# 74 of 4096 attention tiles get their exponential from VectorE's polynomial instead of ScalarE, and LayerNorm's squares go by halves

## The chip, the cores and the metric

The kernel runs on one core of a Trainium2 chip. The core has five engines with a queue of instructions each, which run side by side and wait for one another through semaphores: TensorE (PE in the profile, with its weight loads as PEld), VectorE (DVE), ScalarE (ACT), GpSimd (POOL) and SyncE (SP), whose queue issues most of the DMAs. On-chip memory is SBUF, with 128 partitions, and PSUM, with 8 banks of 128 x 512 fp32, into which TensorE writes. The metric is device time in microseconds of one launch, as the median of several.

## The reference

Two kinds of layer alternate, A, B, A, B, each adding to the stream `x` of 2048 x 1024 bf16, 32 heads of 32.

```python
x = A_x
x = x + _A_ref(_layernorm(x, axis=-1), A_wqkv, A_w_phi, A_wo)   # linear attention
x = x + _B_ref(_layernorm(x, axis=-1), B_wqkv, B_wo)            # softmax attention
x = x + _A_ref(_layernorm(x, axis=-1), A_wqkv, A_w_phi, A_wo)
x = x + _B_ref(_layernorm(x, axis=-1), B_wqkv, B_wo)
...
scores = jnp.einsum("bhqd,bhkd->bhqk", q, k) * (Dh ** -0.5)
p = _softmax(scores, axis=-1)
o = jnp.einsum("bhqk,bhkd->bhqd", p, v)
```

`_A_ref` computes features `softmax(q w_phi)` and `softmax(-q w_phi)`, the same for k, sums `phi_k` times v over the sequence, and divides `phi_q kv` by `phi_q z`. The bulk of the arithmetic on elements is the softmax of `_B_ref`: 32 heads x 2048 x 2048 exponentials, twice.

## The kernel before, in words

`x` stays in SBUF, transposed (`xT`: features on partitions), in four chunks of 512 positions. One A and one B are called a layer here, so the program has two layers.

**Attention** (`attention`). A unit is one tile of scores: 128 keys by 512 queries of one head. A layer has 2048 of them. The order is fixed by `turns`: a turn is one group of four heads (`g`, 8 of them) and one chunk of queries (`qc`, 4), 32 turns a layer, first chunks 0 and 1 alternating over the groups and then chunks 2 and 3. A turn has two halves (`pp`), each with 8 steps `d` of 4 units (`j`, one per row group of TensorE). The units of a layer are taken three at a time:

- L937: three score matmuls (32 rows of the array each) into three PSUM banks, 0 to 2 and 3 to 5 by turns.
- L943: one ScalarE `Exp` over 128 x 1536, from PSUM into one of five SBUF buffers of class `E`.
- L972: for two units, four matmuls on 32 columns each, `v` and a block of ones times the exponentials, accumulated over the half in PSUM bank 6 (`acc`). There is only one `acc`.
- L986: at the end of a half VectorE copies `acc` to SBUF. Two DMAs (L1012 and its neighbour) bring the denominators into place, VectorE takes reciprocals (L1016, four a turn) and multiplies (L1020, two a turn).

Bank 7 (`FIL`) serves everything else that must go on under attention: the projections of later head groups (`b_k`, `b_q`, `q_away`, `b_v`), the output projection (`b_o`, in the second layer `b_last`), and at the end of layer 0 three chunks of the next A (LayerNorm and `a_keys` with `alone=True`). These use the column-tiled matmul of L401, whereas the stages outside attention use the full array, L397.

**LayerNorm** (`layernorm`). Where it is not `alone`: ScalarE squares `xT` in four instructions of 128 x 1024 (L454), each as soon as its quarter of the features is there; ones-matmuls sum `x` and the squares; then L474 and L476 (mean squared, mean), L477 (variance), L479 and L481 (logarithm, exponential), and four pairs of L487 and L491 that write the normalised chunk.

**Order.** `Sched` is a list scheduler that runs while the program is built. Every operation has a priority (`base + 10 * turn + ...`), a modelled duration and buffers taken from one SBUF arena and the PSUM banks with a quota per class. What comes out is one fixed order of instructions for each engine. Where TensorE has nothing to start and has worked less than 75% of the last 3.4 us of the plan, the planner puts in four matmuls of ones times `xT` into bank 7 (`idle`), but only if bank 7 is free. Their result is used by nobody.

Of the kernel before, what the change touches and what calls it, by code (L numbers as in the profile page):

```python
# [9 lines left out]
ACT = mybir.ActivationFunctionType  # L10
ALU = mybir.AluOpType
AX = mybir.AxisListType
BF16 = mybir.dt.bfloat16
F32 = mybir.dt.float32

EPS_LN = 1e-5
# [16 lines left out]
class Op:  # L33
    __slots__ = ("eng", "dur", "lat", "fn", "bufs", "prio", "mode", "ndep", "out", "t", "start", "seq")

    def __init__(self, eng, dur, lat, fn, bufs, prio, mode, seq):
        self.eng, self.dur, self.lat, self.fn, self.bufs = eng, dur, lat, fn, bufs
        self.prio, self.mode, self.seq = prio, mode, seq
        self.ndep, self.out, self.t, self.start = 0, [], 0.0, None

# [5 lines left out]
class Sched:  # L46
    def __init__(self, sbuf_bytes, quota):
        self.ops = []
        self.quota = quota
        self.live = {}  # L50
        self.free = [(0, sbuf_bytes)]
        self.bank_used = [False] * 8
        self.peak = 0
        self.total = sbuf_bytes
        self.queue = {}
        self.idle = None

# [85 lines left out]
    def run(self):  # L143
# [17 lines left out]
        front = 0  # L161
        recent = []
        started = {}
        for o in self.ops:
# [3 lines left out]
        while left:  # L168
            moved = False
            for e in engines:  # L170
# [24 lines left out]
                if e == "PE":  # L195
                    recent.append((t, t + pick.dur))
                d = pick.dur
                if pick.mode is not None:
# [3 lines left out]
                pick.start = t  # L202
                if pick.fn is not self.idle:
                    started[pick.prio] = started.get(pick.prio, 0) + 1
# [44 lines left out]
SPELL = 3.4  # L249
KEEP = 0.75  # L250


def act_us(n):
    return n / 1200 + 0.064
# [10 lines left out]
def kernel(  # L265
# [18 lines left out]
    assert D == 1024 and S % C512 == 0  # L284
    inv_sqrt_dh = float(DH**-0.5)

# [15 lines left out]
    onesD = const.tile([P, P], BF16, tag="onesD")  # L302
    ones_bf = const.tile([P, DH], BF16, tag="ones")
    J_bf = const.tile([P, P], BF16, tag="J")
    ident = const.tile([P, P], BF16, tag="ident")
# [8 lines left out]
    nc.vector.memset(onesD[:], 1.0 / D)  # L314
    nc.vector.memset(ones_bf[:], 1.0)
    nc.vector.memset(J_bf[:], 0.0)
    nc.vector.memset(eps[:], EPS_LN)
# [70 lines left out]
    def csl(c):  # L388
        return slice(c * C512, (c + 1) * C512)
# [48 lines left out]
    def deps_x(c):  # L438
        return list(xdone[c])

    def layernorm(c, prio, banks, alone=False):

# [5 lines left out]
        parts = [deps_x(c)[2 * i:2 * i + 2] for i in range(4)]  # L448
        for h in range(2 if alone else 4):
            hs = slice(4 * h, 4 * h + 4)  # L450
            if not alone:
                hs = slice(2 * h, 2 * h + 2)
                halves.append(op(
                    "ACT", act_us(1024), lambda hs=hs: nc.scalar.activation(  # L454
                        out=xv()[:, hs, :], in_=xT[:, hs, csl(c)], func=ACT.Square),
                    parts[h], [xb], prio))
# [9 lines left out]
        m = mmgroup(mb, mv, lambda po: onesD[:], lambda po: xT[:, po, csl(c)], (), parts, [], prio)  # L466
        q = mmgroup(qb, qv, lambda po: onesD[:], lambda po: xv()[:, po, :], [m],
                    [halves[0], None, halves[1], None] if alone else halves, [xb], prio + 0.01)
        if alone:
# [348 lines left out]
    def b_q(g, c, prio, w, banks):  # L818
        wb, ww, wd = w
        xb, xv, fin = xnB[c]  # L820
        pb, pv = ps("fil", banks)
        m = mmg2(pb, pv, lambda po: ww()[:, po, :], lambda po: xv()[:, po, :], fin, wd, [xb, wb], prio)
        q_b, q_v = sb("q2", 2, C512)
        cp = op("DVE", dve_us(512), lambda: nc.vector.tensor_scalar(
            out=q_v()[:, 0, :], in0=pv(), scalar1=inv_sqrt_dh, scalar2=None, op0=ALU.mult), [m], [pb, q_b], prio)
        return q_b, q_v, q_swap(q_b, q_v, cp, prio)
# [6 lines left out]
    def q_away(g, c, prio, w, banks):  # L833
# [6 lines left out]
        cp = op("DVE", dve_us(512), lambda: nc.vector.tensor_scalar(  # L840
            out=a_v(), in0=pv(), scalar1=inv_sqrt_dh, scalar2=None, op0=ALU.mult), [m], [pb, a_b], prio)
        return dma(prio, lambda: nc.sync.dma_start(out=qd_v[:, c - 2, g, :], in_=a_v()), [cp], [a_b], kb=128)
# [64 lines left out]

    def attention(base, kT, vT, q_of, gate):

# [4 lines left out]
        ]  # L914
        first = {}
        ex_of, e_of = {}, {}
        n = 0
        i = 0
        while i < len(units):
# [14 lines left out]
            def sfn(grp=grp, s_v=s_v):  # L934
# [8 lines left out]
            ex = op("ACT", act_us(w * C512), lambda s_v=s_v, e_v=e_v, w=w: nc.scalar.activation(  # L943
                out=e_v()[:, 0:w * C512], in_=s_v(), func=ACT.Exp), [so], [s_b, e_b], prio - 3)
            for x, u in enumerate(grp):
# [5 lines left out]
        if True:  # L951
            for qc, g in turns:
                T = []
                end = (qc, g) == turns[-1]
                for pp in range(2):
                    a_b, a_v = ps("acc", [(6,)])
                    last = None
                    for d in range(8):
                        prio = base + 10 * pos[(qc, g)] + 5 * pp + 0.5 * d
                        for u in range(2):  # L960
# [18 lines left out]
                            if e_of[us[1]][0] is not ebs[0]:  # L979
                                ebs.append(e_of[us[1]][0])  # L980
                            last = op("PE", 0.225, fn, flat([last, ex_of[us[0]], ex_of[us[1]], v_done[kc % 4]]),
                                      [a_b, v_b, *ebs], prio - 1, mode="c")
                    if end and pp:
                        break
# [67 lines left out]
    for layer in range(2):  # L1052
# [73 lines left out]
        oTs, last_s = attention(at, kT, vT, q_of, gate)  # L1126
        if last:
# [50 lines left out]
    sch.idle = idle  # L1178

    for o in sch.run():  # L1180
        o.fn()
# [30 lines left out]
```

## Time and profile before

| | us |
|---|---|
| median of 3 runs (2552.54 to 2556.16) | 2554.63 |
| the profiled execution | 2554.77 |
| its span | 2553.0 |
| ACT busy | 2181.1 |
| PE busy | 2329.9 |
| DVE busy | 1144.7 |

PE's busy time is modelled from pipelined matmuls and includes the `idle` ones. From about 420 to 1340 us the program is in the first attention, from about 1620 us to the end in the second; before each lies a stage of A with the projections of B.

### The profile page before, as it was taken

To read this page: it belongs to the slowest core of one execution; us is meant where nothing else is said; L and a number is where in the kernel's file an instruction comes from. 1 tells how busy PE (TensorE), PEld (TensorE's weight loads), DVE (VectorE), ACT (ScalarE), POOL (GpSimd) and SP (SyncE) were. 2 spreads that over 40 slices of the span, in tenths; PEclk is the share of its full clock that TensorE was granted. 3 is DMA by queue.
4 is the path that set the end of the run, shared out by engine and by line. 5 is a ranking of instruction groups with operands and counts; after the bars stand their busy time and mean duration, and the time that the engine had idled before them with its cause. 6 is when DMAs were issued, how large, how long until landed. Compare 5 with 4: busy or idle time off the path is not lost.

```text
span 2553.0 us, 60236 instructions
## 1 busy us (share of the span) xinstructions
PE 2329.9 (91%) x26714; PEld 882.9 (35%) x26780; DVE 1144.7 (45%) x1632; ACT 2181.1 (85%) x1945; POOL 25.8 (1%) x72
## 2 busy tenths in 40 slices
PE   6899999999898998899898999999998898889888
PEld 3443443333322333333333344333332233333333
DVE  5997653333322245655646766333333222212124
ACT  5325647999999999999996555799999999999998
POOL 0000000000000000000000000000000000000000
PEclk9999999999998999999999999999999899999999
DMA  9020011111121222222323001111121011001000
GB/s 215 1 75 1 5 38 46 35 35 44 40 64 38 53 53 70 75 64 69 117 71 102 1 5 38 36 45 35 37 67 30 20 33 43 20 18 33 18 20 26
DMA packets 185270, 117.21 MB, mean 46 GB/s; under 512 B 103345, under 2 KB 175025, under 8 KB 184241
## 3 DMA queue, kind: packets, MB, share of 16 engines
q1 hardware_dynamic: 183952, 111.26, 16.3%
q8 instruction: 209, 3.42, 0.6%
q10 hardware_dynamic: 1056, 2.10, 0.2%
q14 instruction: 53, 0.43, 0.1%
HBM read 62.46 MB, written 15.73 MB: 31 GB/s over the span
## 4 chain that ended last, share of the span: by engine, by line
ACT 53%; PE 26%; issue 11%; DVE 8%; SPq 1%; DMA 1%; ACTq 0%; DVEq 0%; another core or an unknown queue 0%
ACT arena L943 51%; PE psum L397 13%; PE psum L401 4%; PE psum L972 3%; PE psum L937 3%; DVE arena L593 2%; DVE arena L602 1%; PE psum L757 1%; DVE arena L491 1%; DVE arena L487 1%; ACT arena L589 1%; SPq L432 1%; DVE arena L596 1%; DVE arena L639 0%; PE psum L702 0%
## 5 line engine op out<-in xcount | busy, mean ns | idle before, releaser
L943 ACT ACTIVATE arena<-psum 128x1536 bf16<-128x1536 f32 (+1 forms) x1366 | 1844.4, 1560 | 29.1 <-PE psum L937 23.6
L972 PE MATMUL psum<-arena 128*32 128x512 bf16 x4096 | 712.7, 390 | 13.5 <-ACT arena L943 11.6
L972 PE MATMUL psum<-arena,ones_bf 128*32 128x512 bf16 x4096 | 714.1, 391 | 0.0
L937 PE MATMUL psum<-arena 32*128 32x512 bf16 x4096 | 537.8, 387 | 135.5 <-ACT arena L943 127.3
L401 PE MATMUL psum<-arena 128*32 128x512 bf16 x8256 | 582.5, 382 | 13.8 <-DVE arena L840 2.1
L397 PE MATMUL psum<-arena 128*128 128x512 bf16 x1973 | 468.6, 382 | 26.5 <-DVE arena L491 5.5
L937 PEld LDWEIGHTS <-arena 32*128 32x128 bf16 x4096 | 181.7, 91 | 643.8 <-issue 632.1
L401 PEld LDWEIGHTS <-arena 128*32 128x32 bf16 x8256 | 213.0, 96 | 222.1 <-issue 74.2
L397 PEld LDWEIGHTS <-arena 128*128 128x128 bf16 x2032 | 193.2, 98 | 268.5 <-issue 50.2
L986 DVE COPY arena<-psum 128x512 f32<-128x512 f32 x126 | 86.9, 690 | 431.3 <-PE psum L972 428.0
L972 PEld LDWEIGHTS <-arena 128*32 128x32 bf16 x4096 | 167.7, 94 | 283.0 <-issue 259.3
L1016 DVE RECIPROCAL arena<-arena 128x128 f32<-128x128 f32 x248 | 212.8, 913 | 85.7 <-DMA arena<-arena 82.8
L816 DVE CAST arena<-psum 128x512 bf16<-128x512 f32 x112 | 77.4, 691 | 283.5 <-PE psum L401 280.3
L972 PEld LDWEIGHTS <-ones_bf 128*32 128x32 bf16 x4096 | 162.1, 94 | 70.1 <-issue 58.7
L401 PE MATMUL psum<-xT,onesD 128*32 128x512 bf16 x2172 | 179.7, 382 | 0.6 <-DVE xT L876 0.3
L589 ACT ACTIVATE arena<-psum 128x512 bf16<-128x512 f32 x80 | 42.6, 603 | 110.7 <-PE psum L397 58.8
L454 ACT ACTIVATE arena<-xT 128x1024 bf16<-128x1024 bf16 x52 | 54.6, 1060 | 73.2 <-DVE xT L792 59.2
L719 ACT ACTIVATE arena<-psum 128x512 bf16<-128x512 f32 x128 | 69.8, 598 | 38.2 <-PE psum L397 32.2
L602 DVE TENSOR_TENSOR arena<-psum,arena 128x1024 bf16<-128x1024 f32 x64 | 78.3, 1224 | 43.6 <-PE psum L401 39.4
L1020 DVE TENSOR_TENSOR arena<-arena 64x512 bf16<-64x512 f32 x124 | 85.0, 686 | 10.1 <-PE psum L972 5.7
L487 DVE TENSOR_TENSOR arena<-xT,arena 128x1024 f32<-128x1024 bf16 x64 | 77.7, 1218 | 22.7 <-ACT arena L476 22.4
L593 DVE TENSOR_REDUCE arena<-arena 128x32 f32<-128x1024 bf16 x64 | 77.6, 1213 | 19.1 <-ACT arena L589 15.0
(89 smaller groups left out, 1051.8 us busy)
## 6 DMA issues: line engine op xcount, KB each, us to landing
arena<-arena SPq DMA_DIRECT2D x124, 128.0 KB, 2.3
arena<-in_A_wqkv_dram SPq DMA_DIRECT2D x10, 1024.0 KB, 5.7
arena<-in_B_wqkv_dram SPq DMA_DIRECT2D x32, 256.0 KB, 3.3
arena<-arena SPq DMA_DIRECT2D x256, 32.0 KB, 1.9
arena<-in_B_wo_dram SPq DMA_DIRECT2D x32, 256.0 KB, 3.1
arena<-wd_k SPq DMA_DIRECT2D x8, 1024.0 KB, 6.1
arena<-in_A_wo_dram SPq DMA_DIRECT2D x4, 1024.0 KB, 6.5
arena<-in_B_wqkv_dram SPq DMA_DIRECT2D x4, 1024.0 KB, 5.5
```

The lines of the kernel that those rows point to most:

```text
L397: nc.tensor.matmul(out_, lhsT=lhsT, rhs=rhs, start=start, stop=stop, skip_group_check=True)
L401: nc.tensor.matmul(out_[ks, :], lhsT=lhsT[:, ks], rhs=rhs, start=start, stop=stop, tile_position=(0, 32 * k), skip_group_check=True)
L487: s1 = op("DVE", dve_us(1024), lambda pr=pr, w_v=w_v: nc.vector.tensor_tensor(out=w_v(), in0=xT[:, pr, csl(c)], in1=m_v().unsqueeze(1).to_ ...
L593: red = op("DVE", dve_us(1024), lambda ev=ev, sv=sv: nc.vector.reduce_sum(out=sv(), in_=ev().rearrange("p s (h d) -> p (s h) d", d=DH), ax ...
L602: ml = op("DVE", dve_us(1024), lambda vpv=vpv, wv_=wv_, sv=sv: nc.vector.tensor_tensor(out=wv_()[:, :, :, 0:DH], in0=vpv().rearrange("p (h ...
L816: return op("DVE", dve_us(512), lambda: nc.vector.tensor_copy(out=dst(), in_=src()), [dep], bufs, prio)
L937: nc.tensor.matmul(out=s_v()[:, x * C512:(x + 1) * C512], lhsT=kT[g][1]()[r, pp, d * P:(d + 1) * P], rhs=q_of[(qc, g)][1]()[r, (pp + j // ...
L943: ex = op("ACT", act_us(w * C512), lambda s_v=s_v, e_v=e_v, w=w: nc.scalar.activation(out=e_v()[:, 0:w * C512], in_=s_v(), func=ACT.Exp), ...
L972: nc.tensor.matmul(out=a_v()[col:col + 32, :], lhsT=v_v()[:, kc % 4, o:o + DH] if what == 0 else ones_bf[:], rhs=ev()[:, x * C512:(x + 1) ...
L986: cp = op("DVE", dve_us(512), lambda t_v=t_v, a_v=a_v: nc.vector.tensor_copy(out=t_v(), in_=a_v()), [last], [a_b, t_b], prio - 4)
L1016: rc = [op("DVE", 128 * 8 / 960 + 0.12, lambda b=b, d_v=d_v, r_v=r_v: nc.vector.reciprocal(out=r_v()[:, b * P:(b + 1) * P], in_=d_v()[:, b ...
L1020: s = [op("DVE", dve_us(512), lambda a=a, b=b, k=k, o_v=o_v, r_v=r_v, T=T: nc.vector.tensor_tensor(out=o_v()[a, :], in0=T[k][1]()[a, :], i ...
```

## The change

- **`exp_dve`.** 37 pairs of units (keys `d` = 2 and 3 of one half, `j` = 3) leave the groups of three. For each unit TensorE writes the scores alone into bank 7 (class `xs`), and VectorE computes the exponential: with the scores scaled by 1/(4 ln 2), the exponential is 2 to the power of four times the score. Adding 1.5 * 2^21 rounds to quarters, a subtraction leaves the rest, a clamp, a conversion to int32 gives the bits of the power of two, and four multiply-adds evaluate a polynomial of degree four in the rest. That is 10 VectorE instructions a pair: four of 128 x 512 with PSUM as a source (L949, L952, twice each), two of 128 x 1024 in SBUF alone (L955, L958), and four of 128 x 1024 with two sources (L963 three times, L966). The result goes into a buffer `E1` of which there are three.
- **`EXTRA`** says which: in layer 0 one pair in each of turns 12 to 16; in layer 1 one pair in turns 8 to 16, 20, 24 and 28, and two pairs in turns 17 to 19, 21 to 23, 25 to 27 and 29. That makes 10 and 64 units.
- `q` is scaled by 1/(4 ln 2) more, and ScalarE's `Exp` gets the constant `scale=4 ln 2`, no bias.
- **`idle_acc`.** Where bank 7 is taken and an accumulation in bank 6 is open, the planner may fill with four matmuls of zeros into `acc`.
- **LayerNorm.** Squares go in two instructions of 128 x 2048, and squares and sums wait for the whole chunk (`deps_x(c)`), except in the one LayerNorm that begins layer 1's A (`n=4`), which keeps quarters.

```diff
+ROUND = 1.5 * 2**21
+LEAD = 5.0
+EXTRA = (lambda i: [(i % 2, 2)] if 12 <= i < 17 else [],
+         lambda i: [(0, 2), (1, 2)] if 16 < i < 30 and i % 4 else [(i % 2, 2)] if 8 <= i < 30 else [])
...
-                    if worked < KEEP * SPELL and not self.live.get("fil", 0) and not self.bank_used[7]:
+                    if worked >= KEEP * SPELL:
+                        pass
+                    elif self.bank_used[7]:
+
+                        if accum:
+                            pick = Op("PE", MM, LAT["PE"], self.idle_acc, (), 0.0, "c", 0)
+                            left += 1
+                    elif not self.live.get("fil", 0):
...
-    def layernorm(c, prio, banks, alone=False):
+    def layernorm(c, prio, banks, alone=False, n=2):
...
-        for h in range(2 if alone else 4):
-            hs = slice(4 * h, 4 * h + 4)
+        for h in range(n):
+            hs = slice(8 // n * h, 8 // n * h + 8 // n)
...
-                    parts[h], [xb], prio))
+                    parts[h] if n == 4 else deps_x(c), [xb], prio))
...
+    def exp_dve(qc, g, pp, d, prio, kT, q_of):
+        u_b, u_v = sb("xu", 2, C512, dt=F32)
+        g_b, g_v = sb("xg", 2, C512, dt=F32)
+        x_b, x_v = sb("xx", 2, C512, dt=F32)
+        e_b, e_v = sb("E1", 2, C512)
+        r = slice(96, 128)
+        gs = []
+        for k in range(2):
+            s_b, s_v = ps("xs", FIL)
...
+            so = op("PE", MM, sfn, flat([kT[g][2][(d + k) // 2], q_of[(qc, g)][2]]),
+                    [s_b, kT[g][0], q_of[(qc, g)][0]], prio, mode="r")
+            uo = op("DVE", dve_us(512), lambda k=k, s_v=s_v: nc.vector.tensor_scalar(
+                out=u_v()[:, k, :], in0=s_v(), scalar1=POW2_D, scalar2=ROUND, op0=ALU.add, op1=ALU.add),
+                [so], [s_b, u_b], prio + 0.01)
+            gs.append(op("DVE", dve_us(512), lambda k=k, s_v=s_v: nc.vector.scalar_tensor_tensor(
+                out=g_v()[:, k, :], in0=u_v()[:, k, :], scalar=ROUND, in1=s_v(), op0=ALU.subtract, op1=ALU.subtract),
+                [uo], [s_b, u_b, g_b], prio + 0.01))
+        wo = op("DVE", 1024 / 1920 + 0.15, lambda: nc.vector.tensor_scalar(
+            out=u_v(), in0=u_v(), scalar1=ROUND - 31.5, scalar2=ROUND + 32.0, op0=ALU.max, op1=ALU.min),
+            gs, [u_b], prio + 0.02)
+        wo = op("DVE", 1024 / 1920 + 0.15, lambda: nc.vector.tensor_scalar(
+            out=u_v().bitcast(I32), in0=u_v(), scalar1=ROUND - 31.75, scalar2=float(2**25),
+            op0=ALU.subtract, op1=ALU.mult), [wo], [u_b], prio + 0.02)
+        last = gs
+        for i, c in enumerate(POW2_C):
+            last = [op("DVE", dve_us(1024), lambda i=i, c=c: nc.vector.scalar_tensor_tensor(
+                out=x_v(), in0=(x_v() if i else g_v()), scalar=c, in1=g_v(), op0=ALU.add, op1=ALU.mult),
+                last, [g_b, x_b], prio + 0.02)]
+        eo = op("DVE", dve_us(1024), lambda: nc.vector.scalar_tensor_tensor(
+            out=e_v(), in0=x_v(), scalar=POW2_0, in1=u_v(), op0=ALU.add, op1=ALU.mult),
+            [wo, *last], [x_b, u_b, e_b], prio + 0.02)
...
             ex = op("ACT", act_us(w * C512), lambda s_v=s_v, e_v=e_v, w=w: nc.scalar.activation(
-                out=e_v()[:, 0:w * C512], in_=s_v(), func=ACT.Exp), [so], [s_b, e_b], prio - 3)
+                out=e_v()[:, 0:w * C512], in_=s_v(), func=ACT.Exp, scale=4 * math.log(2)),
+                [so], [s_b, e_b], prio - 3)
...
-            xnA[c] = layernorm(c, base + 10 * c - 9 if base + c else -16.0, ANY)
+            xnA[c] = layernorm(c, base + 10 * c - 9 if base + c else -16.0, ANY, n=4 if layer else 2)
...
+    def idle_acc():
+        for k in range(4):
+            nc.tensor.matmul(psum[32 * k:32 * k + 32, 6 * C512:7 * C512], lhsT=zero[:], rhs=xT[:, 0, 0:C512],
+                             start=False, stop=False, tile_position=(0, 32 * k), skip_group_check=True)
+    sch.idle_acc = idle_acc
```

More of the change, by code (lines that the diff above doesn't have):

```diff
@@ L33 @@
 class Op:
-    __slots__ = ("eng", "dur", "lat", "fn", "bufs", "prio", "mode", "ndep", "out", "t", "start", "seq")
+    __slots__ = ("eng", "dur", "lat", "fn", "bufs", "prio", "mode", "ndep", "out", "t", "start", "seq", "accum")
     def __init__(self, eng, dur, lat, fn, bufs, prio, mode, seq):
@@ L38, in __init__ @@
         self.prio, self.mode, self.seq = prio, mode, seq
-        self.ndep, self.out, self.t, self.start = 0, [], 0.0, None
+        self.ndep, self.out, self.t, self.start, self.accum = 0, [], 0.0, None, None
 LAT = {"PE": 0.25, "ACT": 0.2, "DVE": 0.1, "POOL": 0.2, "SP": 2.0, "AQ": 2.0}
@@ L315 @@
     nc.vector.memset(ones_bf[:], 1.0)
+    nc.vector.memset(zero[:], 0.0)
     nc.vector.memset(J_bf[:], 0.0)
@@ L911, in attention @@
+    def attention(base, kT, vT, q_of, gate, extra):
         units = [
@@ L914, in attention @@
         ]
-        first = {}
         ex_of, e_of = {}, {}
+        for qc, g in turns:
+            for pp, d in extra(pos[(qc, g)]):
+                eo, (e_b, e_v) = exp_dve(qc, g, pp, d, base + 10 * pos[(qc, g)] + 5 * pp + 0.5 * d - LEAD, kT, q_of)
+                for k in range(2):
+                    ex_of[(qc, g, pp, d + k, 3)] = eo
+                    e_of[(qc, g, pp, d + k, 3)] = (e_b, e_v, k)
+        units = [u for u in units if u not in ex_of]
         n = 0
@@ L1125 @@
                     q_of[(qc, g)] = q_back(g, qc, at + 10 * pos[(qc, g)] - 12, away)
-        oTs, last_s = attention(at, kT, vT, q_of, gate)
+        oTs, last_s = attention(at, kT, vT, q_of, gate, EXTRA[layer])
         if last:
```

33 lines of the change are left out of this document (23 added, 10 removed), and 3 rows, old and new, of the table QUOTA.

## The prediction, written before the changed kernel ran

> **What bounds the kernel now.** I read the page's busy line and slices first, then the chain that ended last, then busy time by stretch, then the waits of the second attention (1620 us to the end) and of the slow spot at 740 to 800 us, and last the groups for the durations.
>
> ```profile
> PE 2329.9 (91%) x26714; PEld 882.9 (35%) x26780; DVE 1144.7 (45%) x1632; ACT 2181.1 (85%) x1945; POOL 25.8 (1%) x72
> ...
> DVE  5997653333322245655646766333333222212124
> ACT  5325647999999999999996555799999999999998
> ...
> ACT 53%; PE 26%; issue 11%; DVE 8%; SPq 1%; DMA 1%; ACTq 0%; DVEq 0%; another core or an unknown queue 0%
> ```
> ```profile
> 760.00:770.00 10.00, 7.63 (x65) 1.70 (x57) 0.69 (x1) 9.18 (x8) 0.00 (x0) 0.74 0.06 13
> 770.00:780.00 10.00, 8.41 (x61) 1.92 (x58) 0.69 (x1) 8.78 (x7) 0.00 (x0) 0.50 0.01 2
> 1850.00:2475.00 625.00, 557.70 (x7449) 194.67 (x7445) 166.54 (x222) 622.29 (x463) 0.00 (x0) 0.99 0.11 31
> ```
> ```profile
> 2436.42 2.64 ACT arena L943 x2
> 2439.11 2.63 ACT arena L943 x2
> 2441.78 2.65 ACT arena L943 x2
> ...
> 380.31 1.06 ACT arena L454
> ```
> ```profile
> PE psum L937 <- ACT arena L943: 66.5, 270, 0.6
> PE psum L972 <- ACT arena L943: 5.4, 23, 0.4
> ...
> PE psum L937 <- ACT arena L943: 6.5, 15, 0.6
> ```
> ```profile
> L943 ACT ACTIVATE arena<-psum 128x1536 bf16<-128x1536 f32 x1364 | 1842.5, 1560 | 29.1 <-PE psum L937 23.6 <-PE psum L972 3.5 <-issue 1.3
> L1016 DVE RECIPROCAL arena<-arena 128x128 f32<-128x128 f32 x248 | 212.8, 913 | 85.7 <-DMA arena<-arena 82.8 <-ACT arena L943 2.4
> L986 DVE COPY arena<-psum 128x512 f32<-128x512 f32 x126 | 86.9, 690 | 431.3 <-PE psum L972 428.0 <-DMA arena<-arena 3.0
> L487 DVE TENSOR_TENSOR arena<-xT,arena 128x1024 f32<-128x1024 bf16 x64 | 77.7, 1218 | 22.7 <-ACT arena L476 22.4
> L687 DVE SCALAR_TENSOR_TENSOR arena<-arena,hl 128x512 bf16<-128x512 bf16 x32 | 24.0, 751 | 1.2
> L840 DVE TENSOR_SCALAR arena<-psum 128x512 bf16<-128x512 f32 x32 | 22.1, 691 | 85.3 <-PE psum L401 80.1 <-DMA arena<-arena 5.0
> L686 DVE CAST arena<-arena 128x512 bf16<-128x512 f32 x32 | 13.6, 425 | 38.8 <-ACT arena L775 34.3 <-ACT arena L742 4.4
> ```
>
> In both attentions ScalarE is full and VectorE mostly idle. The stretch 1850 to 2475 holds 44 of the copies of L986, so it is turns 8 to 29 of layer 1: ScalarE works 622.3 of 625 us, VectorE 166.5 (7.6 us a turn). The chain there is exponentials end to end, two groups in 2.69 us. TensorE waits for ScalarE before the scores (66.5 us in all, 0.6 us at most), and its 558 us include filling. So a unit costs 2.69/6 = 0.448 us of the end time, and every unit taken off ScalarE there gives that back unless something else comes late.
>
> **The change, part by part.**
>
> *Exponentials that leave ScalarE.* 74 units x 0.448 = **-33.2 us** (28.7 in layer 1, 4.5 in layer 0). All lie in turns where ScalarE is the bound. The constant scale costs nothing: L589 has one and takes 603 ns, as L719 does (598) and the scale-free Square of L474 (598).
>
> *The polynomial on VectorE.* Per pair: L949 twice as L840, 2 x 0.69; L952 twice between L477 (0.686) and L687 (0.751), 2 x 0.72; four of 1024 elements with two sources as L487, with up to 0.065 more as L687 has over L477, 4 x 1.25; L955 and L958 have no row. Their bounds are 0.425 (L686, fp32 from SBUF, one source, half the elements) and 1.22 (L487); L686 runs at about half the time per element of L477, which over 1024 elements gives about 0.69, and it is their nearest row, so 2 x 0.69. Sum 9.2 us, ends 8.5 and 10.5. 37 x 9.2 = 340 us of VectorE. Beside ScalarE that costs nothing as long as a turn of VectorE is shorter than a turn of ScalarE. With two pairs: 7.6 + 18.4 = 26.0 us against 60 x 0.448 = 26.9; with one: 16.8 against 27.8. So ten turns of layer 1 are 97% full on VectorE, and only the one-pair turn after each three leaves slack, 11 us. Three `E1` buffers let VectorE run ahead by no more than three pairs; in the changed order most pairs end between the copies of the two halves before their use.
>
> What queues behind: VectorE works in order, so copies of `acc` (L986, now L1057), reciprocals and the evacuations of bank 7 wait for the polynomial step in front, 1.25 us at most each. 39 of the 126 copies stand directly behind a polynomial step. For the copy waits the next half's accumulation on TensorE (one `acc`), and behind that, in TensorE's order, the next scores. Two score buffers give ScalarE 1.34 us of cover beyond the group it is in. I take 0.6 us lost in each of the ten two-pair turns: **+6 us**. Ends: 0 (all covered) and +22 (10.5 us a pair makes such turns 28.6 us, 1.7 over, ten times, plus 5 for copies).
>
> *Scores for VectorE.* 74 single matmuls of at most 0.39 us each (the length of one in L937) against 25 groups of three less, and 792 fills of four matmuls for 519 by the two orders, at 0.216 us each (the page's chain has 32 of L401 in 1.73): about +75 us of TensorE. Cost 0: they lie in TensorE's waits for ScalarE and in place of each other. Without that cover a single score would be some 0.3 us late, 74 times, under the 22 us above.
>
> *Fills while bank 7 is taken.* At 740 to 800 us bank 7 is held, nothing fills, and the granted clock falls to 0.50; ScalarE loses 0.82 and 1.22 us in the two slices shown. The slices of 10 us with a clock under 0.95 (700, 760 to 800, 1910 to 1930, 1980 to 2020) lose 7.4 us of ScalarE together. The zero matmuls should hold the clock where `acc` is open. I take a little over half, **-4 us**; ends -7.4 and +3 (new low spots where the copy is late, no accumulation is open and bank 7 is held). The Trainium skill (TensorE: Matmul & The Clock Gate, "HAM oscillation") says that the clock halves after an idle window of about 3.4 us. By it nothing would have throttled here, since TensorE waited 0.6 us at most, this term would be 0 and the sum 2528.6. The trace disagrees: 0.50 at 770 to 780 with matmuls every 1.4 us, and the measurement decides.
>
> *LayerNorm.* Two squares of 2048 cost about 1.9 each (1.06 plus 1024 elements at the 0.82 ns that L943's 1560 and 1139 for 512 fewer give), back to back 3.7 for 3.9. But all now follow the last addition, where only one of 1.06 did: 2.7 us later. That is on the path for the last chunk of each layer's B LayerNorm (the chain has 380.31 L454, and attention cannot run freely before 400 us); the others lie under the next chunk's queries. In return, in the order of the changed kernel six exponentials stand in that gap instead of three, 4.0 us of ScalarE's later work, two of them between the mean and the logarithm. I take 0 for each gap, ends -2 and +6 for both, and **+1 us** for the kernel's start, where the first LayerNorm must wait for all eight loads (ends -3 and +5; the weights' folding runs there until 41 us).
>
> SP's and GpSimd's queues issue the same instructions, 739 and 74, and nothing is moved past them but by the planner's own shifts.
>
> **Sum** against the profiled execution's own 2554.77 (the median is 2554.63, the same): 2554.8 - 33.2 + 6 - 4 + 1 = 2524.6, so 2524 us.
>
> **The rivals.**
> - *VectorE bounds the two-pair turns.* For it: 97%, and steps without a row. If L955 and L958 take 1.22 us, a pair costs 10.3, the ten turns 28.2 us for 26.9 (+13), with copies late +5; -33.2 + 18 - 2 + 1 gives 2538, up to 2549. Against it: the one-pair turns' slack. By the rows a unit is ten times dearer on VectorE (4.6 us for 0.448), which matters only from the point where VectorE is full. The Trainium skill (ScalarE: Activation LUTs, "Rules for kernel authors") calls ScalarE the only option for `exp`; it speaks against this change and leads to this rival.
> - *All of it goes through*, and the clock holds: -33.2 - 7.4 - 1, 2513. For it: TensorE's waits for ScalarE all over 1850 to 2475.
> - *Slower: the single `acc` starves ScalarE.* A copy behind two or more polynomial steps (2.5 us, plus its own 0.69) exceeds the 1.34 us of cover, and ScalarE loses about 1 us in each of the 54 halves of the turns concerned: 2554.8 - 33.2 - 4 + 1 + 54 = 2573. It decides from (33.2 + 4 - 1)/54 = 0.67 us a half. For it: today VectorE idles 428 us waiting for TensorE before L986, so copies have never been late. Against it: it needs more than one step ahead of nearly every copy, and copies have the earlier priority.
> - *Nothing gained*: the lost time at that price, within 5 us of 2555.
>
> **How the numbers follow.** A measurement of this kernel tells about 0.2%, 5 us, from no change. Forecast (2512 to 2537) 0.60, VectorE bound (2537 to 2549) 0.19, better than 2512 0.06, unchanged 0.03, slower 0.12. Faster 0.85. The range leaves out the slower, the unchanged and the best: 2511 to 2549.
>
> **What would show it.** L1012 at 1342 groups or so with the same 1.344 us pitch; about 601 us (625 - 28.7 + 6 - 2 for the clock) where turns 8 to 29 of layer 1 took 625 (if 612 or more, VectorE or the copies took it, and ScalarE's waits name L1006 or L1042); VectorE near 26 of 27 us in turns 17 to 19; L955 and L958 near 0.69 us; no slice under 0.9 of the clock in the attentions; L477's 1.9 us and attention starting some 3 us later, with six groups done. Wrong it would be if ScalarE shows waits of over 0.5 us at every half, or if VectorE's steps depend on each other at more than their own length.

## The result: 2510.6 us for 2555.4, and the profile after

The changed kernel takes 2510.62 us (median of 4 runs, 2506.32 to 2512.10) against 2555.39 (2552.54 to 2556.66) for the kernel before: a ratio of 0.9824, 95% interval 0.9807 to 0.9841. It is faster by 44.8 us. The forecast was faster by 31, 2524, with a range of 2511 to 2549: the time lies 0.4 us under the range's lower end. The profiled execution of the changed kernel took 2511.27, its span is 2509.5.

The page's busy line, the slices of VectorE, ScalarE and TensorE's clock, and the chain that ended last, of the kernel after:

```profile
PE 2368.6 (94%) x27872; PEld 893.4 (36%) x27872; DVE 1468.5 (59%) x2003; ACT 2145.4 (85%) x1897; POOL 26.1 (1%) x72
...
DVE  6997653333356345654646766333356578687854
ACT  6335558999999999999996465699999999999998
...
PEclk9999999999999999999999999999999999999999
...
ACT 46%; PE 31%; issue 12%; DVE 8%; SPq 1%; DMA 1%; ACTq 0%; DVEq 0%
```

VectorE has 324 us more, most of it in the last third, and ScalarE's row of nines in the second attention is as long as it was. The work moved as planned. Busy time by stretch, in the columns of the prediction (PE, PEld, DVE, ACT, POOL, clock, DMA share, GB/s), first where the clock had been 0.74 and 0.50, then 598 us out of turns 8 to 29 of layer 1:

```profile
760.00:770.00 10.00, 9.75 (x134) 3.58 (x135) 9.38 (x11) 10.00 (x9) 0.00 (x0) 1.00 0.42 126
770.00:780.00 10.00, 9.51 (x144) 3.50 (x140) 4.66 (x7) 10.00 (x8) 0.00 (x0) 1.00 0.11 30
1835.00:2433.00 598.00, 558.24 (x7603) 190.74 (x7599) 435.40 (x531) 590.86 (x440) 0.00 (x0) 0.99 0.12 32
```

The last stretch begins 4 us later in its turns than the prediction's stretch of 625 us did. Measured between the same two copies of `acc`, the first and the last that the 625 us held, 620.1 us (1850.6 to 2470.7) became 596.7 (1830.7 to 2427.4). That is 23.4 less, which puts 601.6 where 625 stood; the prediction said about 601. So the error of the forecast lies for the most part outside this stretch. ScalarE has 10 of 10 us where it had 9.18 and 8.78. In the 598 us, the waits that matter:

```profile
PE psum L1006 <- ACT arena L1012: 32.0, 90, 3.7
...
ACT arena L1012 <- DMA qd<-arena: 3.6, 1, 3.6
...
PE psum L1042 <- DVE arena L1057: 1.5, 5, 0.5
```

The accumulations waited for VectorE's copy of `acc` for 1.5 us in 22 turns: the copies are not late. One exponential waited 3.6 us for the store of a query tile, which no step of the prediction has. The groups with the new work, by shape:

```profile
L1012 ACT ACTIVATE arena<-psum 128x1536 bf16<-128x1536 f32 x1340 | 1811.4, 1567 | 50.5 <-PE psum L1006 43.7 <-DMA qd<-arena 3.6 <-PE psum L1042 1.2
L949 DVE TENSOR_SCALAR arena<-psum 128x512 f32<-128x512 f32 x74 | 51.0, 690 | 62.5 <-PE psum L944 54.3 <-PE psum L1006 6.2 <-ACT arena L1012 1.9
L966 DVE SCALAR_TENSOR_TENSOR arena<-arena 128x1024 bf16<-128x1024 f32 x37 | 45.3, 1225 | 4.5 <-PE psum L1042 0.9 <-DVE arena L963 0.4 <-DMA arena<-qd 0.2
```

and the two that had no row before, by line (shortest, median and longest in ns):

```profile
L955 DVE TENSOR_SCALAR arena<-arena x37: 683/693/696, 700.0 to 2405.4; 128x1024 f32<-128x1024 f32 x37
L958 DVE TENSOR_SCALAR arena<-arena x37: 682/694/697, 700.7 to 2406.1; 128x1024 int32<-128x1024 f32 x37
```

**Where the 43.6 us lie.** The copies of `acc` (L986, now L1057) mark the halves of the turns in both traces (turn 7.5 is the copy after the second half of turn 7, turns counted from 0), and the first reciprocals of `a_keys` (L596, now L619) mark the start of the first stage. After minus before:

| mark | us |
|---|---|
| first reciprocal of `a_keys` | -9.2 |
| layer 0, first copy of `acc` | -12.2 |
| layer 0, turn 7.5 | -10.4 |
| layer 0, turn 16.5 | -20.2 |
| layer 0, last copy | -19.2 |
| layer 1, turn 7.5 | -19.9 |
| layer 1, turn 9 | -15.0 |
| layer 1, last copy | -43.6 |

So about 10 us are won before any attention has begun, where the prediction had a loss of 1, and some are lost again at turn 8 of layer 1.

### The profile page after: what moved, and what is told of

It is laid out like the page before. It is cut to its first block, busy times and chain, and to the rows that moved or that the text cites. A ratio compares the mean times of both kernels' runs of the same rounds, so it can differ in the third digit from the quotient of the medians.

```text
span 2509.5 us, 62924 instructions
## 1 busy us (share of the span) xinstructions
PE 2368.6 (94%) x27872; PEld 893.4 (36%) x27872; DVE 1468.5 (59%) x2003; ACT 2145.4 (85%) x1897; POOL 26.1 (1%) x72
## 4 chain that ended last, share of the span: by engine, by line
ACT 46%; PE 31%; issue 12%; DVE 8%; SPq 1%; DMA 1%; ACTq 0%; DVEq 0%
ACT arena L1012 43%; PE psum L421 14%; PE psum L425 5%; PE psum L1042 5%; PE psum L1006 4%; DVE arena L616 1%; SPq L456 1%; PE psum L1253 1%; PE psum L780 1%; ACT arena L612 1%; DVE arena L625 1%; DVE arena L963 1%; DVE arena L662 1%; DVE arena L510 1%; DVE arena L514 1%
## 5 line engine op out<-in xcount | busy, mean ns | idle before, releaser
L1012 ACT ACTIVATE arena<-psum 128x1536 bf16<-128x1536 f32 x1342 | 1812.4, 1566 | 50.5 <-PE psum L1006 43.7
L1042 PE MATMUL psum<-arena 128*32 128x512 bf16 x4096 | 699.0, 385 | 11.6 <-ACT arena L1012 8.4
L1042 PE MATMUL psum<-arena,ones_bf 128*32 128x512 bf16 x4096 | 700.3, 386 | 0.0
L1006 PE MATMUL psum<-arena 32*128 32x512 bf16 x4022 | 522.8, 383 | 74.6 <-ACT arena L1012 68.3
L425 PE MATMUL psum<-arena 128*32 128x512 bf16 x8256 | 576.3, 380 | 4.9 <-DVE arena L625 1.3
L421 PE MATMUL psum<-arena 128*128 128x512 bf16 x2032 | 474.2, 383 | 18.1 <-DVE arena L514 5.4
L1006 PEld LDWEIGHTS <-arena 32*128 32x128 bf16 x4022 | 163.4, 91 | 574.8 <-issue 564.9
L1253 PE MATMUL psum<-xT,zero 128*32 128x512 bf16 x2712 | 218.5, 382 | 0.0
L839 DVE CAST arena<-psum 128x512 bf16<-128x512 f32 x112 | 77.3, 690 | 238.5 <-PE psum L425 238.1
L1057 DVE COPY arena<-psum 128x512 f32<-128x512 f32 x126 | 86.8, 689 | 157.3 <-PE psum L1042 155.6
L963 DVE SCALAR_TENSOR_TENSOR arena<-arena 128x1024 f32<-128x1024 f32 x111 | 135.6, 1222 | 2.3
L612 ACT ACTIVATE arena<-psum 128x512 bf16<-128x512 f32 x80 | 42.8, 600 | 86.1 <-PE psum L421 57.8
L625 DVE TENSOR_TENSOR arena<-psum,arena 128x1024 bf16<-128x1024 f32 x64 | 78.3, 1224 | 39.6 <-PE psum L425 35.5
L1253 PEld LDWEIGHTS <-zero 128*32 128x32 bf16 x2712 | 70.3, 97 | 64.5 <-issue 16.8
L514 DVE TENSOR_TENSOR arena<-arena 128x1024 bf16<-128x1024 f32 x64 | 77.4, 1223 | 23.9 <-ACT arena L504 22.6
```

The source lines that it names most:

```text
L421: nc.tensor.matmul(out_, lhsT=lhsT, rhs=rhs, start=start, stop=stop, skip_group_check=True)
L425: nc.tensor.matmul(out_[ks, :], lhsT=lhsT[:, ks], rhs=rhs, start=start, stop=stop, tile_position=(0, 32 * k), skip_group_check=True)
L514: fin.append(op("DVE", dve_us(1024), lambda pr=pr, w_v=w_v: nc.vector.tensor_tensor(out=xv()[:, pr, :], in0=w_v(), in1=r_v().unsqueeze(1). ...
L625: ml = op("DVE", dve_us(1024), lambda vpv=vpv, wv_=wv_, sv=sv: nc.vector.tensor_tensor(out=wv_()[:, :, :, 0:DH], in0=vpv().rearrange("p (h ...
L963: last = [op("DVE", dve_us(1024), lambda i=i, c=c: nc.vector.scalar_tensor_tensor(out=x_v(), in0=(x_v() if i else g_v()), scalar=c, in1=g_ ...
L1006: nc.tensor.matmul(out=s_v()[:, x * C512:(x + 1) * C512], lhsT=kT[g][1]()[r, pp, d * P:(d + 1) * P], rhs=q_of[(qc, g)][1]()[r, (pp + j // ...
```

## The experiments

The change has three parts: the polynomial, the zero matmuls and the halves of LayerNorm. The first seven runs take it apart. Line numbers in traces of other kernels can differ by a few; they are named by what they do.

**The zero matmuls alone** (of the changed kernel's parts; no polynomial, and quarters everywhere but in the LayerNorms under attention, `alone`, which have two parts in every kernel).

```diff
-EXTRA = (lambda i: [(i % 2, 2)] if 12 <= i < 17 else [],
-         lambda i: [(0, 2), (1, 2)] if 16 < i < 30 and i % 4 else [(i % 2, 2)] if 8 <= i < 30 else [])
+EXTRA = (lambda i: [], lambda i: [])
...
-    def layernorm(c, prio, banks, alone=False, n=2):
+    def layernorm(c, prio, banks, alone=False, n=4):
...
-            xnA[c] = layernorm(c, base + 10 * c - 9 if base + c else -16.0, ANY, n=4 if layer else 2)
+            xnA[c] = layernorm(c, base + 10 * c - 9 if base + c else -16.0, ANY)
```

> The kernel before with the zero matmuls alone: no polynomial (all exponentials on ScalarE), quarters in every LayerNorm. The prediction's theory (the zero matmuls give back what ScalarE lost in the low spots of the clock of before, 7.4 us, and nothing more): 2547 to 2551. Rival 1 (without the polynomial's score tiles in bank 7 the old fills do as well, and the zero matmuls are worth nothing): 2553 to 2556. Rival 2 (the 17.9 us of the kernel without polynomial are mostly the zero matmuls, the start's 10 us being lost again as in the kernel with the LayerNorm's edit alone): 2537 to 2541. If the start's gain survives only with a held clock, the time is near 2547 and the 17.9 us are a sum of about 7.4 and 10.4.

Measured: 2546.91, ratio to the kernel before 0.9968 (95% interval 0.9955 to 0.9980): 7.8 us. By the copies it is level at turn 9 of layer 0, 5.7 us ahead at turn 15, 4.7 at turn 7.5 of layer 1, 8.4 at turn 13.5 and 8.3 at the end: the gain comes in the two stretches where the clock of before was low. So the term for the clock is at the end that the prediction gave it, -7.4, and not a little over half of it.

**LayerNorm's halves alone**, on the kernel before.

```diff
-        for h in range(2 if alone else 4):
-            hs = slice(4 * h, 4 * h + 4)
+        for h in range(n):
+            hs = slice(8 // n * h, 8 // n * h + 8 // n)
...
-                    parts[h], [xb], prio))
+                    parts[h] if n == 4 else deps_x(c), [xb], prio))
...
-            xnA[c] = layernorm(c, base + 10 * c - 9 if base + c else -16.0, ANY)
+            xnA[c] = layernorm(c, base + 10 * c - 9 if base + c else -16.0, ANY, n=4 if layer else 2)
```

> The kernel before with the LayerNorm edit alone. The traces put the first 10.4 us of the gain ahead of the first copy of acc, where no polynomial runs. If it is the LayerNorm edit (theory 1): 2545 us, first statistics of a_keys at 37 us instead of 47, attention of layer 1 starting at the same lead. If the gain at the start came from the planner's order being shifted by other parts (theory 2), or as the prediction has it: 2554 to 2557.

Measured: 2552.60, ratio 0.9993 (0.9984 to 1.0002): nothing that can be told from none. But the way there is not nothing (its profiled execution, 2557.05, is the longest of the ten). The start wins 7.9 at the first reciprocal, and at turn 27 of layer 0 the lead is 10.1. Then 3.6 go at turn 28, 4.5 are left at turn 7.5 of layer 1, and at its turn 18 the kernel is 1.6 behind. At turn 28 of layer 0 it is a late DMA. From 1218 to 1280 us of this kernel:

```profile
DVE arena L1015 <- DMA arena<-arena: 4.6, 1, 4.6
ACT arena L942 <- PE psum L936: 4.6, 4, 2.2
...
PE psum L401 <- DVE arena L585: 2.4, 1, 2.4
```

A reciprocal on VectorE (L1015) waits 4.6 us for the copy of the denominators. Next in VectorE's order stands an evacuation of the next A (L585), TensorE waits 2.4 us for that, and ScalarE for the scores (L936) that TensorE then does late. In layer 1 it is the clock, which is lower than before. Busy time of 1980 to 2000 us in this kernel,

```profile
1980.00:2000.00 20.00, 17.85 (x147) 4.27 (x150) 2.08 (x3) 17.39 (x14) 0.00 (x0) 0.57 0.08 20
```

and in the kernel before:

```profile
1980.00:2000.00 20.00, 16.31 (x158) 4.52 (x158) 2.77 (x4) 18.48 (x14) 0.00 (x0) 0.74 0.09 20
```

A clock of 0.57 for 0.74, and ScalarE's 18.48 of 20 us became 17.39. From 1640 us on, ScalarE is idle for 6.8 us in the slices of 10 us with a clock under 0.95, and for 2.3 us in the kernel before. So part of the lead goes at the late DMA, and 4.5 of the 6.1 us lost after turn 7.5 of layer 1 go in new low spots of the clock.

**The change without LayerNorm's part** (quarters everywhere).

```diff
-    def layernorm(c, prio, banks, alone=False, n=2):
+    def layernorm(c, prio, banks, alone=False, n=4):
...
-            xnA[c] = layernorm(c, base + 10 * c - 9 if base + c else -16.0, ANY, n=4 if layer else 2)
+            xnA[c] = layernorm(c, base + 10 * c - 9 if base + c else -16.0, ANY)
```

> The changed kernel with quarters in every LayerNorm, so polynomial and zero fills alone. Theory 1: 2521 us (2510.6 + 10.4), the prediction's sum without its start term (2524 - 1 = 2523). Theory 2, the start gain has nothing to do with LayerNorm: 2511.

Measured: 2518.95, ratio 0.9861 (0.9846 to 0.9876), 8.3 us more than with it. Beside zero matmuls most of the start's gain stays: of 11.6 us between the two kernels at the first copy, 6.5 are left at the last.

**Which chunks of the start.** Two kernels made from the one before, with one run each: halves for chunks 1 to 3 of layer 0's A alone (the edit shown), and halves for the LayerNorms of B alone.

```diff
-            xnA[c] = layernorm(c, base + 10 * c - 9 if base + c else -16.0, ANY)
+            xnA[c] = layernorm(c, base + 10 * c - 9 if base + c else -16.0, ANY, n=2 if layer == 0 and c else 4)
...
-            xnB[c] = layernorm(c, pr + 23, ANY)
+            xnB[c] = layernorm(c, pr + 23, ANY, n=4)
```

> The kernel before with halves in the LayerNorms of chunks 1 to 3 of layer 0's A alone. In before their squares stand in ScalarE's queue ahead of the first exponential of a_keys (44.3 us), in the changed kernel only one does (35.1 us). If that order is the gain at the start (theory 1): first exponential at 35 to 40 us, first copy of acc 5 to 10 us earlier than 412.3. If it is the first chunk's own LayerNorm (theory 2): unchanged, 44 and 412.

> The kernel before with halves in the B LayerNorms alone. The prediction takes 0 per layer (2.7 us of latency against three more exponentials in the gap), ends -2 and +6: start unchanged, the first copy of acc within 2 us of 412.3, and the time in the two gaps unchanged to some 2 us. Theory 2: the latency shows, +3 us at each layer's first copies.

Measured: 2555.11 with chunks 1 to 3, first exponential of `a_keys` at 36.67 us, first reciprocal 7.7 us earlier and first copy 5.8 earlier, all of it lost again later (7 at turn 28 of layer 0, where the reciprocal waits 7.4 us for the same late copy of the denominators). 2554.39 with B's, first copy 1.8 earlier, then 0.3; before layer 1's attention the lead falls from 3.7 to 1.9. So the two gaps before attention cost 0 to 2 us, near the 0 that was predicted. Of LayerNorm's gain at the start, 7.9 us at the first reciprocal of layer 0 and 8.5 at its last, chunks 1 to 3 alone give 7.7 and 6.2: most of it comes from them and not from chunk 0. ScalarE's timeline shows why. Before (start, us, line, and how many):

```profile
32.28 2.02 ACT L454 ACTIVATE arena<-xT 128x1024 bf16<-128x1024 bf16 x2
...
34.84 3.90 ACT L454 ACTIVATE arena<-xT 128x1024 bf16<-128x1024 bf16 x4
...
42.43 2.04 ACT L454 ACTIVATE arena<-xT 128x1024 bf16<-128x1024 bf16 x2
44.33 1.11 ACT L589 ACTIVATE arena<-psum 128x512 bf16<-128x512 f32 x2
```

After:

```profile
32.72 1.91 ACT L477 ACTIVATE arena<-xT 128x2048 bf16<-128x2048 bf16 x1 [3.26 <-DMA xT<-in_A_x_dram]
34.61 0.59 ACT L570 CAST arena<-psum 128x512 bf16<-128x512 f32 x1
35.09 2.07 ACT L612 ACTIVATE arena<-psum 128x512 bf16<-128x512 f32 x4
...
40.24 1.91 ACT L477 ACTIVATE arena<-xT 128x2048 bf16<-128x2048 bf16 x1 [1.67 <-DMA xT<-in_A_x_dram]
```

With quarters, squares of later chunks can start as soon as a part of `x` is loaded, and the planner sets them ahead: eleven squares of 1024 stand between 30.57 and 44.33 us in front of the first exponential of `a_keys` (L589), and among them the copies of the weights' folding (L547, now L570). With halves that need a whole chunk, one square of 2048 stands there and the exponentials (L612) begin at 35.09. The `a_keys` that follow keep the lead: -9.2 at the first reciprocal, -11.4 at the last.

**The change without the polynomial.**

> The changed kernel without any polynomial unit: LayerNorm edit, scale in the exponential and zero fills. Theory 1 with a polynomial worth 28 us net (33.2 less stalls): 2538 to 2540. If VectorE's load costs most of the 33.2 us (rival of the prediction): under 2530. If the units bring all of 33.2: 2544.

```diff
-EXTRA = (lambda i: [(i % 2, 2)] if 12 <= i < 17 else [],
-         lambda i: [(0, 2), (1, 2)] if 16 < i < 30 and i % 4 else [(i % 2, 2)] if 8 <= i < 30 else [])
+EXTRA = (lambda i: [], lambda i: [])
```

Measured: 2537.42, ratio 0.9934 (0.9919 to 0.9949). From the zero matmuls alone (2546.91) to this: 9.5 us for LayerNorm. From this to the whole change (2510.62): 26.8 us for the polynomial. The prediction had 33.2 - 6 = 27.2 us for it.

**The change without the zero matmuls.**

```diff
                     elif self.bank_used[7]:
-                        if accum:
+                        if False:
```

> The changed kernel without the zero matmuls into the open accumulation. If they hold the clock (theory 1): slices with a clock under 0.9 come back, above all in turns 17 to 29 of layer 1 where bank 7 is held by the score tiles, and the time is 2515 to 2535. If the clock needs no fills there (theory 2, the polynomial's own scores are work enough): within 3 us of 2510.

Measured: 2536.34, ratio 0.9925 (0.9908 to 0.9941): 25.7 us more than with them, though alone they give 7.8. Busy time of 605 us out of turns 8 to 29 of layer 1 in this kernel, and one stretch in it; then what TensorE waited for from 2100 to 2130:

```profile
1835.00:2440.00 605.00, 522.17 (x6031) 161.48 (x6028) 432.15 (x527) 584.02 (x431) 0.00 (x0) 0.88 0.12 31
2110.00:2120.00 10.00, 8.98 (x69) 2.06 (x71) 6.14 (x9) 9.01 (x8) 0.00 (x0) 0.63 0.07 16
```
```profile
PE psum L1006 <- ACT arena L1012: 2.8, 6, 0.6
PE psum L1042 <- ACT arena L1012: 1.0, 3, 0.4
```

The mean clock is 0.88 for 0.99, and ScalarE is idle for 21 us of 605, for 7 of 598 in the change. The score tiles of the polynomial hold bank 7, and while it is held the old fills can't run. TensorE's longest wait at the clock of 0.63 is 0.6 us, so it is not one long pause that lowers it. The Trainium skill has this case too, beside the rule that the prediction weighed (TensorE: Matmul & The Clock Gate, "A second HAM failure mode: psum-queue depth-cycling"): short idle moments between groups of matmuls are enough to make the clock go down and up. The trace agrees: 0.63 with no wait over 0.6 us. Not all of the 25.7 us come from the polynomial. Between LayerNorm's halves alone (2552.60) and the kernel without the polynomial (2537.42), which adds the zero matmuls to them, lie 15.2 us; some 10 more come with the polynomial. Seen from the other side, the polynomial gives 16.3 us without the zero matmuls (2552.60 to 2536.34) and 26.8 with them. So the zero matmuls are not an extra of 4 us: the other two parts give much less without them.

**More on VectorE: two pairs in every turn from 8 to 29 of layer 1** (12 pairs more).

```diff
-         lambda i: [(0, 2), (1, 2)] if 16 < i < 30 and i % 4 else [(i % 2, 2)] if 8 <= i < 30 else [])
+         lambda i: [(0, 2), (1, 2)] if 8 <= i < 30 else [])
```

> The changed kernel with two pairs in each of the turns 8 to 29 of layer 1 (44 pairs for 32), which makes every such turn 97% full on VectorE by the prediction's price and takes away the one-pair turns' slack. If VectorE keeps up (theory 1): 24 more units x 0.448 us are gained, about 2500 us. If VectorE is the bound at two pairs (the prediction's rival): no gain beyond a few us, or a loss, with ScalarE waiting for TensorE's scores throughout: 2508 to 2530.

Measured: 2520.71, ratio 0.9864 (0.9848 to 0.9881): 10.1 us more than the change, where 24 units at 0.448 would have given 10.8 less. Busy time of the stretch and ScalarE's and TensorE's waits in it:

```profile
1835.00:2440.00 605.00, 556.84 (x7779) 196.29 (x7771) 532.89 (x644) 580.39 (x430) 0.00 (x0) 1.00 0.12 32
```
```profile
ACT arena L1012 <- PE psum L1006: 23.4, 30, 1.9
...
PE psum L1042 <- DVE arena L1057: 2.9, 6, 0.6
```

VectorE is at 88%, ScalarE loses 24.6 us, and it is the scores (L1006) that are late, 30 times. TensorE itself waits for VectorE only a little: its waits in this stretch for L1057, L839 and L952 are 4.5 us in sum. The scores are late because they stand late in TensorE's fixed order: at 1985.0 us there are 32 matmuls of a projection (1.95 us) in front of them, at 2199.5 another 32 (2.05 us). That the planner put them there because its own VectorE was full is an argument, not a measurement. So with 24 units more a loss appears as the prediction's first rival, no slack on VectorE, would have it; that VectorE's lack of slack is its cause is not shown.

**The wait at turn 8 of layer 1.** ScalarE's timeline of the change, and SyncE's queue:

```profile
1836.68 16.29 ACT L1012 ACTIVATE arena<-psum 128x1536 bf16<-128x1536 f32 x12
1856.62 4.13 ACT L1012 ACTIVATE arena<-psum 128x1536 bf16<-128x1536 f32 x3 [3.65 <-DMA qd<-arena]
```
```profile
1847.15 1.31 SPq L522 DMA_DIRECT2D arena<-in_B_wo_dram  x2
1848.57 1.11 SPq L865 DMA_DIRECT2D qd<-arena  x1
```

TensorE in the meantime:

```profile
1858.12 0.39 PE L1006 MATMUL psum<-arena 32*128 32x512 bf16 x3 [3.73 <-ACT arena L1012]
...
1862.44 0.61 PE L1006 MATMUL psum<-arena 32*128 32x512 bf16 x3
...
1865.24 0.40 PE L1006 MATMUL psum<-arena 32*128 32x512 bf16 x3
```

The store of a query tile (L865) was issued at 1848.57 behind two weight loads (L522) and still held back an exponential at 1856.6, 8 us later. The second of these loads landed at 1856.20, the store at 1856.51; the median of the 32 such stores is 1.8 us from issue to landing. The planner reckons with 2.64 us, after which it gives the tile's SBUF to someone else, here the buffer of an exponential. TensorE then stands for 3.73 us, and its granted clock is 0.50 from 1860 to 1865 (0.61 us a matmul for 0.39). Here the rule that the prediction cited (the same page of the Trainium skill, "HAM oscillation") does fit: an idle window over 3.4 us, and the clock halves. The kernel with quarters has a wait of this kind at the same turn, on VectorE: a copy (L839) waits 8.6 us for a store that took 7.7 us to land. Two runs take the wait away with a longer modelled store, in both layers and in the second alone.

```diff
-        return dma(prio, lambda: nc.sync.dma_start(out=qd_v[:, c - 2, g, :], in_=a_v()), [cp], [a_b], kb=128)
+        return dma(prio, lambda: nc.sync.dma_start(out=qd_v[:, c - 2, g, :], in_=a_v()), [cp], [a_b], kb=1400)
```

> The changed kernel with one number of the planner changed: the store of a query tile to HBM is given 9 us instead of 2.64 until its SBUF buffer may be used again. At turn 8 of layer 1 an exponential waited 3.65 us for such a store, the clock fell behind it, and the lead over before shrank by 8 us. If that wait is the cause (theory 1): no wait for the store, no drop of the lead at turn 8, 2503 to 2507 us. If the 8 us come from the first polynomial pair itself, which starts at turn 8 too (theory 2): the drop stays, 2510.

Measured: 2505.99, ratio 0.9808 (0.9793 to 0.9822). The loss at turn 8 of layer 1 is gone, but the plan of layer 0 became another one and lost 4 us at its turn 28 (a reciprocal there waits 5.0 us for the denominators, as in the kernel with the halves alone).

> The changed kernel with the planner's 9 us for the store of a query tile (for 2.64) in the second layer alone. Every engine's order of instructions is that of the changed kernel; only the places of tiles in SBUF differ, from the first store of layer 1 on. Theory (an exponential of turn 8 waits because it was given the SBUF space of a query tile that a store still reads; the order has no part in it): the loss of 8 us at turn 8 of layer 1 is gone, the loss of 4 us that the first kernel with 9 us had at turn 28 of layer 0 does not come, and the time is 2500 to 2504. Rival (the first such kernel avoided the loss because its order in layer 0 was another one, and the space has no part in it): the wait at turn 8 stays and the time is 2508 to 2512.

Measured: 2502.64 (2501.27 to 2504.66), ratio 0.9792 (0.9776 to 0.9809), 8 us below the change and faster than both kernels. Every engine's order is that of the change; only places in SBUF differ. 596 us out of turns 8 to 29 of layer 1:

```profile
1828.00:2424.00 596.00, 560.32 (x7690) 192.63 (x7686) 438.02 (x534) 595.97 (x445) 0.00 (x0) 1.00 0.12 33
```

ScalarE works 595.97 of 596 us. At the last copy this kernel is 52.2 us ahead of before. With the same order on VectorE there is next to no stall, so what the change lost in the stage was not copies behind polynomial steps. By the copies of the two traces, 6.1 of the 8.6 us between them arise at turn 8, at the store, and 1.6 at turn 20. The cause of the latter stays open.

**More in layer 0.** On the last kernel, one pair in each of turns 10 to 24 of layer 0 for 12 to 16 (the edit shown), and then in turns 9 to 17 (`9 <= i < 18`).

```diff
-EXTRA = (lambda i: [(i % 2, 2)] if 12 <= i < 17 else [],
+EXTRA = (lambda i: [(i % 2, 2)] if 10 <= i < 25 else [],
```

> The kernel with the planner's 9 us in the second layer, and twenty more units for VectorE in layer 0: one pair in each of turns 10 to 24 where it was 12 to 16. In that stretch ScalarE is at 48 to 50 of 50 us and VectorE at 16 to 38. Theory (while ScalarE is full and VectorE has room, a unit is worth its whole 0.448 us): 20 x 0.448 = 9.0 us less, 2492 to 2496. Rival 1 (layer 0's bank 7 has the next projections and output to serve, and the score tiles delay these): less than half of the gain, 2498 to 2503. Rival 2 (a new plan brings new waits, as the first kernel with 9 us had): slower, 2504 or more.

Measured: 2533.77, ratio 0.9917 (0.9900 to 0.9933), 31 us worse. Against the kernel it is built on it is 4.5 us ahead at turn 18 and 32 us behind at turn 27. ScalarE's waits from 955 to 1240 us:

```profile
ACT arena L1012 <- PE psum L1006: 13.8, 15, 3.3
ACT arena L1012 <- PE psum L1042: 11.1, 3, 5.2
ACT arena L612 <- DVE arena L609: 9.2, 2, 8.4
ACT arena L1012 <- DVE arena L966: 8.9, 2, 4.6
```

From turn 18 on the next A runs under attention (L609, L612, L616, L625), on VectorE and in bank 7. Now exponentials of attention wait for the polynomial's last step (L966), and that A's exponentials (L612) for VectorE's evacuations (L609): the longest wait, 8.4 us, ends at 1110.16, where the evacuation stands behind the ten steps of a pair (1099.62 to 1109.5). VectorE is busy for 169 of 250 us from 1000 to 1250, and for 147 in the kernel it is built on. An average share that leaves room did not say that there was room at the right moment.

> As the kernel with twenty more units in layer 0, but only in turns 9 to 17 (eight more units than 12 to 16 gives), so that no polynomial stands in the turns from 18 on, where VectorE also works for the next layer's A. Theory (the twenty units were worth their 0.448 us each up to turn 18, 4.5 us by the copies of the two traces, and the loss of over 30 us came only from the polynomials beside the next A): 2502.6 - 8 x 0.448 = 2499, that is 2497 to 2501. Rival (any new plan of layer 0 brings waits at its end): 2503 or more.

Measured: 2499.34 (2498.99 to 2504.19), ratio 0.9796 (0.9780 to 0.9812). By the copies it is 3.6 us ahead of the kernel it is built on, which is 8 x 0.448; by their ratios to the kernel before, 0.9796 and 0.9792, the two can't be told apart.

## Why the prediction was right or wrong

- **The bound and the price of a unit: right.** 0.448 us for each of 74 units was to give 33.2. Without the polynomial the last copy is 17.9 us ahead, with it and without the store's wait 52.2: 34.3. The stretch of 625 us became 601.6, for about 601.
- **The polynomial on VectorE: right.** L949 0.690, L952 0.687, L955 and L958 0.693, L963 1.222, L966 1.225: a pair is 9.03 us, for 9.2. The two lines without a row came out at the value that L686 led to. VectorE in the full turns 17 to 19 was to be near 26 of 27 us; 2090 to 2117 has 23.5, and the fullest stretch, 25.6, stands among the one-pair turns (2017 to 2044).
- **Copies behind polynomial steps, +6: the size was right and the cause wrong.** TensorE waited 1.5 us for the copies. The change lost 8.6 us against the same order without the store's wait, most of it (6.1) at one place, through a tile of SBUF that was given away before its store was done. With that taken away the term is 0, its lower end.
- **The clock, -4: too small.** It is -7.8 alone, a little past its end of -7.4. That end left out two slices with a clock of 0.83 (at 930 and 1070 us, 0.49 and 0.41 us of ScalarE); with them it is -8.3, which is what the copies show for the zero matmuls alone. And one thing was missed: the polynomial takes bank 7 from the old fills, so that without the zero matmuls the same kernel loses 25.7 us, where halves without the polynomial would lose 15.2. The end of +3 for new low spots was far from what they would have cost.
- **LayerNorm, +1: the step that failed.** The prediction reasoned on the first chunk, which "must wait for all eight loads", and gave the start -3 to +5. The runs give -8.3 (the change against quarters) and -9.5 (added to the zero matmuls). What it missed is the queue: the squares of chunks 1 to 3 stand in ScalarE's order ahead of the first exponentials, and those went from 44.33 to 35.09 us. This term alone is about 10 of the 13 us by which 2524 was too high; the clock is the other 4. The size of the term is not LayerNorm's alone: without the zero matmuls the same edit gives 2 us that can't be told from none, since the lead of the start is lost again under attention. The two gaps before attention were near 0, as taken: from the last reciprocal of A to turn 1.5 of attention it is 0.9 us longer in layer 0 and 0.6 shorter in layer 1, and not 3 us later.
- **The sum, with what was measured:** 2554.8 - 33.2 + 8.6 - 7.8 - 9.5 = 2512.9; the profiled execution took 2511.3.
- **The rivals.** The slower one needed 0.67 us a half for `acc`; 1.5 us in 44 halves rules it out. VectorE as the bound did not come in this change. A little further on, with the pairs beside the next A, other work waits for it; with two pairs in all turns a loss came too, whose cause is not shown. "All of it goes through", 2513, is where the time came out, but by luck: the change did lose 8.6, which that rival had at 0, and LayerNorm paid for it. The Trainium skill's word that ScalarE is the only option for `exp` (ScalarE: Activation LUTs, "Rules for kernel authors") is not borne out here: 74 of 4096 units on VectorE gave 26.8 us, for as long as VectorE had time.

## What to carry to other kernels

When an instruction becomes able to start earlier or only later, look at what stands behind it in its engine's order, not only at what it waits for itself: here eleven early squares kept the first exponentials back by 9 us. An edit's parts need not add up: the halves gave 2 us alone, not to be told from none, and 8 to 10 beside the zero matmuls; the zero matmuls gave 8 alone, 15 beside the halves and 26 beside halves and polynomial. And when an exponential waits for a DMA that only stores, ask who held its buffer before: a longer modelled store in the second layer, with no instruction moved, gave 8 us.

## What the runs showed of the hardware that was not expected

- A store of a 128 x 512 bf16 tile, issued behind two loads of weights, still held its source buffer 8 us after its issue (1848.57 to 1856.6), where the plan has 2.64 and the median of such stores is 1.8.
- Without the zero matmuls the granted clock fell to 0.63 in a stretch in which TensorE never waited longer than 0.6 us, and over 605 us to a mean of 0.88. With matmuls that have an operand of zeros it was 0.99 to 1.00 there, at 382 ns each like others.
- An fp32 to int32 conversion of 128 x 1024 in SBUF on VectorE takes the same 693 ns as a clamp in fp32, little over half of the 1222 ns of the step with two sources.
